# First projections taken by weight piece, no filler matmuls, chunk 1's input turned by DMA, score runs joined, and a new order for a fused attention and ReGLU block

## The chip, the cores and the metric

One core of a Trainium2 chip runs the kernel. The metric is the device time in microseconds (us) of one execution; the kernel before has a median of 191.26 us over three runs (191.16 to 192.79). The engines are PE (matmul), DVE (vector), ACT (scalar activation, which also copies PSUM to SBUF here), POOL (here mostly the issuer of accumulating DMAs) and SP (issuer of the other DMAs). Each engine works through its own instructions strictly in the order of the program and waits on semaphores for the others.

## What is computed

```python
def _A_ref(x, wqkv, wo):                      # S = 2048 tokens, D = 512, 32 heads of 16
    q, k, v = ...                             # x @ wqkv, by heads
    off = jnp.arange(8) * 2                   # each token sees 8 tokens: 0, 2, ... 14 back
    kg, vg = k[..., idx_c, :], v[..., idx_c, :]
    logits = jnp.einsum("bhsd,bhswd->bhsw", q, kg) * scale
    attn = _softmax(where(mask, logits, -1e9))
    o = jnp.einsum("bhsw,bhswd->bhsd", attn, vg)
    return o @ wo
def _B_ref(x, W_gate, W_up, W_down):          # F = 1376
    return (relu(x @ W_gate) * (x @ W_up)) @ W_down
h  = x + _A_ref(_layernorm(x), wqkv, wo)
h2 = h + _B_ref(_layernorm(h), W_gate, W_up, W_down)
```

All tensors are bf16; the sums in PSUM are fp32.

## The kernel before

**Tiling.** The 2048 tokens are four chunks of 512, called 0 to 3. For each chunk the work is: layer norm of x (statistics on DVE, L467 and L470; Ln and Exp for the reciprocal root on ACT, L480 and L484; the normalised row in token order, L515 on DVE for chunk 0 and L512 on ACT for the rest), four tokens-by-features blocks of 128 rows, called x0 to x3 of the chunk; the turn to features-by-tokens, either on PE against an identity (L544) with a copy out of PSUM (L560 on ACT, L558 on DVE for one block), or by a transposing DMA from SP (L533); twelve projection groups of 4 x 512 columns (L585: four for q, four for k with `wqk_sb`, four for v with `wv_sb`), copied out by ACT (L593); the products of q with the eight shifted k on DVE (L636, and L651 in halves for chunk 0; L680 adds two of them beforehand); the scores as column-tiled matmuls against `sel` (L642, L694); Exp (L708); the denominator (L725, L731, L734); the weights scaled by its reciprocal (L752) and spread over the partitions by DMA (L768), four transfers from SP or POOL for each half of the eight offsets; the products with v on DVE (L800, L815), whose sum is begun by an accumulating DMA from POOL (L843) and ended on DVE (L803, L837, L807); the output projection (L881), the residual (L892), the second layer norm (L457, L510, turned by DMA at L533); gate and up (L954, the last 96 features in L921), their product (L982) and down (L1005).

**The start.** The loads of x0 to x3 of chunk 0 and of the q/k weight come in pieces: SP issues x0, x2, x3 and x4, ACT issues x1 and the first three of the four row blocks of the weight (pieces 0 to 2), SP later the fourth. PE runs 77 matmuls on zeros meanwhile (L428), and 8 more behind the turn of x1 (L436, the fillers). The first six of the twelve groups of chunk 0 are issued in parts of 128 or 256 columns and of two weight pieces at a time, so that each part waits only for the columns and the pieces that it reads.

**What sets the order.** A planner (`Plan`) holds every step with its engine, an estimated time and what it needs; the list `RANK` gives each step its place. Loads that the planner does not issue have estimated arrival times in `XT` (x) and `WT` (weights). Its estimates set no waits on the chip: they only choose the order of each engine's instructions and the buffers. Nearly everything that follows, then, is `RANK`.

**Late loads.** `LATE = "ud"` names weights that the planner loads: up and down, behind chunk 0's attention (`lg`, L861). The down loads have one more condition in the plan, chunk 1's spreads (`op.deps += abd`). The gate weights are loaded in the setup (L349).

Of the kernel before, what the change touches and what calls it, by code (L numbers as in the profile page):

```python
# [201 lines left out]
def kernel(  # L202
# [24 lines left out]
    PRE2 = ()  # L227
    PRD = ()
    ODA = (0, 1)
    LATE = "ud"  # L230
    NAB = 0
    SCALE = DH ** -0.5
    EPS = 1e-5
# [72 lines left out]
    def f_load(n, i):  # L306
        if n == "d":
# [3 lines left out]
            if FTAIL and i:  # L311
                nc.sync.dma_start(wd_sb[:FTAIL, NFF, :], B_W_down[NFF * P:F, :])
# [76 lines left out]

    MERGE = (0, 1, 2, 3)  # L390

    BCN = 4

    HG = ([[0, 1, 2, 3]],) * 4
    HSP = ()
# [699 lines left out]
```

## Time and profile before

| | us |
|---|---|
| median of the three runs (lowest, highest) | 191.26 (191.16, 192.79) |
| span of the profiled execution, first to last instruction | 190.2 |
| PE busy | 185.1 (97%) |
| DVE busy | 150.7 (79%) |
| ACT busy | 113.5 (60%) |
| POOL busy | 25.2 (13%) |

The profile is of one execution; its span is 1.06 us under the median of the runs, and the runs do not list the profiled one apart. PE is busy from the first microsecond to 187.3, but "busy" holds the 85 matmuls on zeros, and the end of each matmul is modelled with its latency. DVE is full up to about 125 us and light after that. ACT is nearly full between 16 and 38 us. The granted clock of PE reads 1.00 in every slice of the page but the last.

### The profile page before, as it was taken

The numbers are of one execution on the slowest core, as the hardware profiler recorded it, in microseconds if no ns is written. First come the engines' busy times: TensorE is split into PE (matmuls) and PEld (weight loads), VectorE is DVE, ScalarE is ACT, GpSimd is POOL, SyncE is SP. The second block draws the span as 40 slices with busy tenths as digits, with TensorE's granted clock in tenths as the row PEclk, the third lists the DMA queues.
The fourth block names the chain that finished last, engine by engine and source line by source line (L and its number), as shares of the span: only waits on it lengthen the run. The fifth ranks groups of instructions, "written<-read, shape, count | busy, mean of one in ns | idle before, by whom it ended". The sixth has DMA issues, their size and how long they took to land.

```text
span 190.2 us, 3080 instructions
## 1 busy us (share of the span) xinstructions
PE 185.1 (97%) x1127; PEld 95.4 (50%) x1127; DVE 150.7 (79%) x231; ACT 113.5 (60%) x234; POOL 25.2 (13%) x47
## 2 busy tenths in 40 slices
PE   7799999999999999999999999999999999999993
PEld 7676555554444445544344464444454444455453
DVE  5899999999999999999999998998485712114324
ACT  2579999985467945762483795146466713358500
POOL 4000221400000004230033123027000000000000
PEclk9999999999999999999999999999999999999999
DMA  5999364993198858998438798779922211000503
GB/s 182 281 347 370 90 163 87 191 194 59 21 330 177 233 166 153 194 191 182 83 65 152 142 181 186 180 137 166 221 44 55 55 28 59 28 0 0 165 3 110
DMA packets 27743, 26.98 MB, mean 142 GB/s; under 512 B 14704, under 2 KB 23248, under 8 KB 27728
## 3 DMA queue, kind: packets, MB, share of 16 engines
q1 hardware_dynamic: 23696, 15.34, 29.7%
q0 software_dynamic: 3312, 10.49, 28.6%
q10 hardware_dynamic: 720, 0.95, 1.5%
q8 instruction: 9, 0.15, 0.3%
q14 instruction: 6, 0.05, 0.1%
HBM read 8.42 MB, written 2.10 MB: 55 GB/s over the span
## 4 chain that ended last, share of the span: by engine, by line
PE 82%; ACT 11%; DMA 3%; DVE 1%; issue 1%; SPq 0%
PE bank L954 37%; PE bank L1005 20%; PE bank L585 12%; PE bank L881 7%; ACT row L512 5%; DMA x_sm<-in_A_x_dram 3%; PE bank L921 3%; ACT quad L560 2%; ACT vT L593 2%; PE bank L642 2%; ACT quad L593 1%; PE bank L694 1%; ACT kT L593 1%; ACT ex L708 1%; SPq L323 0%
## 5 line engine op out<-in xcount | busy, mean ns | idle before, releaser
L954 PE MATMUL bank<-quad,wgu_sb 128*128 128x512 bf16 x320 | 72.3, 379 | 0.0
L954 PEld LDWEIGHTS <-wgu_sb 128*128 128x128 bf16 x320 | 30.9, 98 | 37.3 <-issue 1.7
L1005 PE MATMUL bank<-wd_sb,gT 128*128 128x512 bf16 (+3 forms) x198 | 39.7, 355 | 0.0
L958 ACT CAST up_sb<-bank 128x512 bf16<-128x512 f32 x40 | 23.1, 591 | 21.0 <-PE bank L954 14.9
L585 PE MATMUL bank<-quad,wqk_sb 128*128 128x512 bf16 (+2 forms) x176 | 30.4, 321 | 0.5 <-DVE quad L558 0.4
L961 ACT ACTIVATE gr<-bank 128x512 bf16<-128x512 f32 x40 | 23.3, 606 | 9.7 <-PE bank L954 8.2
L1005 PEld LDWEIGHTS <-gT 128*128 128x128 bf16 (+1 forms) x198 | 18.5, 98 | 19.7
L982 DVE TENSOR_TENSOR gT<-gr,up_sb 128x1024 bf16<-128x1024 bf16 x20 | 13.6, 686 | 14.4 <-PE bank L1005 7.0
L636 DVE TENSOR_TENSOR big<-quad,kT 128x4096 bf16<-128x4096 bf16 x11 | 24.8, 2279 | 0.0
L585 PEld LDWEIGHTS <-wqk_sb 128*128 128x128 bf16 x176 | 17.1, 113 | 11.4 <-issue 1.1
L800 DVE TENSOR_TENSOR big<-big,vT 128x4096 bf16<-128x4096 bf16 x9 | 20.4, 2281 | 0.0
L843 POOL DMA_DIRECT2D big<-big x13 | 11.6, 965 | 64.3 <-PE bank L954 32.6
L1013 DVE SCALAR_TENSOR_TENSOR row<-bank,iv,x_sm 128x512 bf16<-128x512 f32 (+2 forms) x10 | 6.3, 643 | 13.4 <-PE bank L1005 13.2
L457 ACT ACTIVATE junk<-x_sm,sm 128x512 bf16<-128x512 bf16 x16 | 11.6, 727 | 8.8 <-DVE x_sm L892 8.8
L585 PE MATMUL bank<-quad,wv_sb 128*128 128x512 bf16 x64 | 16.1, 380 | 0.2 <-ACT quad L560 0.2
L881 PE MATMUL bank<-wo_sb,quad 128*128 128x512 bf16 x64 | 15.0, 379 | 0.0
L892 DVE SCALAR_TENSOR_TENSOR x_sm<-x_sm,bank 128x512 bf16<-128x512 bf16 x16 | 10.8, 678 | 2.4 <-PE bank L881 2.4
L803 DVE TENSOR_TENSOR big<-big 128x1024 bf16<-128x1024 bf16 (+1 forms) x17 | 10.3, 622 | 1.6 <-DMA big<-big 1.4
L467 DVE BATCH_NORM_STATS2 st<-x_sm 128x6 f32<-128x512 bf16 x16 | 10.2, 679 | 1.1 <-DMA x_sm<-in_A_x_dram 1.1
L593 ACT CAST quad<-bank 128x512 bf16<-128x512 f32 x16 | 9.3, 594 | 2.5 <-PE bank L585 2.4
L593 ACT CAST kT<-bank 128x512 bf16<-128x512 f32 x16 | 9.3, 596 | 1.9 <-PE bank L585 1.0
L593 ACT CAST vT<-bank 128x512 bf16<-128x512 f32 x16 | 9.1, 610 | 2.1 <-PE bank L585 2.1
(80 smaller groups left out, 175.6 us busy)
## 6 DMA issues: line engine op xcount, KB each, us to landing
big<-big POOLq DMA_DIRECT2D x13, 512.0 KB, 5.2
big<-ex SPq DMA_DIRECT2D x20, 128.0 KB, 3.1
big<-ex POOLq DMA_DIRECT2D x12, 128.0 KB, 3.8
wgu_sb<-in_B_W_gate_dram SPq DMA_DIRECT2D x1, 1376.0 KB, 9.3
wgu_sb<-in_B_W_up_dram SPq DMA_DIRECT2D x2, 688.0 KB, 5.0
wd_sb<-in_B_W_down_dram SPq DMA_DIRECT2D x2, 640.0 KB, 5.7
x_sm<-in_A_x_dram SPq DMA_DIRECT2D x2, 512.0 KB, 6.2
wqk_sb<-wqk_sb POOLq DMA_DIRECT2D x2, 512.0 KB, 5.8
```

Of the source, the lines that this page charges most:

```text
L457: nc.scalar.activation(out=junk[:, j % 2, :], in_=h.t[:] if h else x_sm[:, tk * BPC + j, :], func=ACT.Square, bias=sm.t[:, j:j + 1], scale ...
L585: nc.tensor.matmul(mm.t[:, lo:hi], lhsT=wv_sb[:, dt, t:D:NT] if c == 2 else wqk_sb[:, dt, c * D + t:(c + 1) * D:NT], rhs=xnT.t[:, dt, lo:h ...
L593: nc.scalar.copy(out=o, in_=mm.t[:])
L636: V.tensor_tensor(out=pb.t[:].rearrange("p (t w) s -> p t w s", t=2), in0=q4, in1=k4, op=ALU.mult)
L800: V.tensor_tensor(out=mt.t[:], in0=ab.t[:], in1=v8, op=ALU.mult)
L843: nc.gpsimd.dma_start(mt.t[:, 0:4, :], mt.t[:, 4:8, :], accum_op=ALU.add)
L881: nc.tensor.matmul(od.t[:], lhsT=OT.t[:, t, j * P:(j + 1) * P], rhs=wo_sb[:, t, :], start=(t == 0), stop=(t == NT - 1 and tk not in RPE))
L954: nc.tensor.matmul(mm.t[:fs, lo:hi], lhsT=wgu_sb[:, dt, g, ft * P: ft * P + fs], rhs=hnT.t[:, dt, lo:hi], start=(dt == 0), stop=(dt == NT ...
L958: nc.scalar.copy(out=ub.t[:fs, i, :], in_=um.t[:fs, :])
L961: nc.scalar.activation(out=gr.t[:fs, i, :], in_=gm.t[:fs, :], func=ACT.Relu)
L982: V.tensor_tensor(out=gt.t[:fs, 0:n, :], in0=gr.t[:fs, 0:n, :], in1=ub.t[:fs, 0:n, :], op=ALU.mult)
L1005: nc.tensor.matmul(od.t[:, c0:c1], lhsT=gts[ft].t[:fs, ft % 2, j * P:(j + 1) * P], rhs=wd_sb[:fs, ft, c0:c1], start=(ft == 0), stop=(ft == ...
```

## The change

Six things, of which the last moves nearly every row.

1. The first six groups of chunk 0 are issued in smaller parts: the first 128 columns with weight piece 0 alone ("a"), then piece 1 ("f"), the next 128 columns with pieces 0 and 1 ("d"), and 256 columns with piece 2 ("g") and piece 3 ("h"). Each part waits in the plan for the piece that it reads (`WP`).
2. The eight fillers are gone (`NFILL`).
3. The copy of the turned x1 goes from DVE to ACT (`TEV = ()`).
4. The normalised rows of chunk 1 are turned by four transposing DMAs on SP instead of 16 PE transposes and two ACT copies (`('x',1,0)` and `('x',1,2)` in `DMAT`).
5. The two score runs of a chunk are issued as one, in chunks 1 to 3 (`MS`).
6. The gate load becomes a planned step (`LATE = "udg"`); the down loads lose their condition (`LDD = 0`); the arrival estimates and `RANK` are new.

```diff
-    LATE = "ud"
+    LATE = "udg"
...
+        elif n == "g":
+            nc.sync.dma_start(wgu_sb[:, :, 0, :], B_W_gate.rearrange("(dt p) f -> p dt f", p=P))
...
-        nc.sync.dma_start(wgu_sb[:, :, 0, :], B_W_gate.rearrange("(dt p) f -> p dt f", p=P))
-
+        if "g" not in LATE:
+            f_load("g", 0)
...
-    NWARM, NFILL = (62, 15), (8, 0, 0)
+    NWARM, NFILL = (62, 15), (0, 0, 0)
...
-    XT = (3.45, 3.65, 4.05, 5.3, 7.15, 8.65, 9.0, 9.4, 13.0, 14.5)
-    WT = (8.35, 8.35, 7.0, 10.85, 15.8, 25.5, 19.2, 29.0)
-    DMAT = (('h',0,0),('h',0,2),('h',2,0),('h',2,2),('h',3,0),('h',3,2),('h',1,0),('h',1,2),('x',3,0),('x',3,2))
+    QD = 6
+    XT = (3.5, 3.7, 4.6, 6.3, 7.3, 8.3, 8.6, 8.95, 13.1, 14.5)
+    WT = (7.95, 7.95, 6.2, 11.2, 15.8, 25.5, 19.2, 29.0)
+    WP = (4.4, 6.2, 7.15, 7.95)
+    DMAT = (('h',0,0),('h',0,2),('h',2,0),('h',2,2),('h',3,0),('h',3,2),('h',1,0),('h',1,2),('x',1,0),('x',1,2),('x',3,0),('x',3,2))
...
+    MS = (1, 2, 3)
+    LDD = 0
...
+    TEV = ()
...
-                tev = not residual and tk == 0 and j0 == 1
+                tev = not residual and tk == 0 and j0 in TEV
...
-                parts = [("a", 0, P, 0, 2, xev[0:1]), ("d", P, 2 * P, 0, 2, xev[1:2])] if n < QA else [("a", 0, 2 * P, 0, 2, xev[0:2])]
-                parts += [("b", 0, 2 * P, 2, NT, [])]
+                if n < QD:
+                    parts = [("a", 0, P, 0, 1, xev[0:1]), ("f", 0, P, 1, 2, []), ("d", P, 2 * P, 0, 2, xev[1:2]), ("g", 0, 2 * P, 2, 3, []), ("h", 0, 2 * P, 3, 4, [])]
...
-                            evs + [wload["ab"][0] if i in "ad" else wl, a, fills[-1]], pr - 5,
+                            evs + wpc[d0:d1] + [a, fills[-1]], pr - 5,
...
+                if tk in MS:
+                    both.append((sc, ex, [a], [prd[0][1]], nu, f_sc))
...
+            elif tk in MS:
+                both.append((sc, ex, [a for a, _, _ in prd], [b for _, b, _ in prd], 4, lambda p=prd: [f() for _, _, f in p]))
...
+            if tk in MS and hf == 0:
+                continue
+            if tk in MS:
+                a = add(("sc1", tk), "PE", sum(x[4] for x in both) * MM + SW, lambda p=both: [x[5]() for x in p],
+                        [d for x in both for d in x[2]], apr, take=[x[0] for x in both], use=[d for x in both for d in x[3]], lat=PEL)
...
-        if tk == 1 and "d" in LATE:
+        if tk == 1 and "d" in LATE and LDD:
             for op in wload["d"]:
                 op.deps += abd
```

How the order moves is read from the two programs themselves. In the rows, `x_sm` is the input, `st` and `mv` the statistics, `rs` the reciprocal root, `row` a normalised block.

**The start on DVE.** Before, the piece with the first normalised rows (`row_104` is x0, `row_105` x1, `row_106` x2, `row_107` x3; `st_116` is the statistic of x3):

```order
L467 BN_STATS st_114<-x_sm 128x6
L470 BN_AGGR mv_117<-st_114 128x2
L515 TENSOR_SCALAR row_104<-x_sm,mv_117,rs_129 128x512
L467 BN_STATS st_115<-x_sm 128x6
L515 TENSOR_SCALAR row_105<-x_sm,mv_117,rs_129 128x512
L470 BN_AGGR mv_117<-st_115 128x2
L467 BN_STATS st_116<-x_sm 128x6
L470 BN_AGGR mv_117<-st_116 128x2
L558 COPY quad_79<-bank_140 128x4x128
L515 TENSOR_SCALAR row_106<-x_sm,mv_117,rs_129 128x512
```

And in the changed program:

```order
L480 BN_STATS st_115<-x_sm 128x6
L483 BN_AGGR mv_117<-st_114 128x2
L483 BN_AGGR mv_117<-st_115 128x2
L528 TENSOR_SCALAR row_104<-x_sm,mv_117,rs_129 128x512
L480 BN_STATS st_116<-x_sm 128x6
L483 BN_AGGR mv_117<-st_116 128x2
L528 TENSOR_SCALAR row_105<-x_sm,mv_117,rs_129 128x512
L528 TENSOR_SCALAR row_106<-x_sm,mv_117,rs_129 128x512
L528 TENSOR_SCALAR row_107<-x_sm,mv_117,rs_129 128x512
```

The row of x1 stood ahead of the statistic of x3 and stands behind it now; the row of x0 stands behind the statistic of x2.

**The start on PE.** In the changed program the end of the turn of x2 and the first projections stand so (`bank` are PSUM banks, `quad_79` is the turned x of chunk 0):

```order
L557 LDWEIGHTS row2_106
L557 MATMUL bank3_141<-identity_61,row2_106 128x128
L598 LDWEIGHTS wqk_sb_72
L598 MATMUL bank4_142<-quad0_79,wqk_sb_72 128x128
L598 LDWEIGHTS wqk_sb_72
L598 MATMUL bank5_143<-quad0_79,wqk_sb_72 128x128
```

Before, fourteen projection matmuls stood ahead of the turn of x2; now the turns of x0, x1 and x2 all stand ahead of the first one.

**Chunk 1's weights on DVE.** Before, the piece from the scaling of the weights (L752; `ex_102` and `ex_100` are the two halves, which the spreads then copy) to the first product with v (L800):

```order
L636 TENSOR_TENSOR big_92<-quad_87,kT 128x4096
L752 TENSOR_TENSOR ex_102<-ex_102,rec_103 128x512
L752 TENSOR_TENSOR ex_100<-ex_100,rec_103 128x512
L636 TENSOR_TENSOR big_89<-quad_87,kT 128x4096
L636 TENSOR_TENSOR big_88<-quad_87,kT 128x4096
L636 TENSOR_TENSOR big_90<-quad_87,kT 128x4096
L680 TENSOR_TENSOR big_92<-big_92,big_88 128x4096
L800 TENSOR_TENSOR wqk_sb<-big_91,vT 128x4096
```

And in the changed program:

```order
L653 TENSOR_TENSOR big_88<-quad_87,kT 128x4096
L783 TENSOR_TENSOR ex_102<-ex_102,rec_103 128x512
L653 TENSOR_TENSOR big_91<-quad_87,kT 128x4096
L783 TENSOR_TENSOR ex_100<-ex_100,rec_103 128x512
L653 TENSOR_TENSOR big_92<-quad_87,kT 128x4096
L697 TENSOR_TENSOR big_88<-big_88,big_91 128x4096
L1013 TENSOR_TENSOR gT_93<-gr_112,up_sb_109 128x1024
L831 TENSOR_TENSOR wqk_sb<-big_89,vT 128x4096
```

Between the second scaling and the first product stood four instructions of 4096 elements; now there stand two, and one of 1024. On SP the down loads follow chunk 1's eight spreads in both programs.

More of the change, by code (lines that the diff above doesn't have):

```diff
@@ L419 @@
         wload[n] = []
+    wpc = [load(t) for t in WP]
     wload["q"][0].take.append(qkb)
@@ L430 @@
     fills = [add(("warm", 0), "PE", 5.6, f_warm, [], -500, take=[wb])]
+    if "g" in LATE:
+        wload["g"].append(add(("ldg", 0), "SP", 0.45, lambda: f_load("g", 0), wload["o"], 0, lat=1.0, dq=(1.0, 3.6)))
     def fill(d, k):
@@ L510, in f_xn @@
                     V.tensor_scalar(out=xn.t[:], in0=x, scalar1=float(D), scalar2=sm.t[:, j:j + 1], op0=ALU.mult, op1=ALU.subtract)
-                elif on_act:
+                elif on_act and (ln, tk, j) not in XND:
                     nc.scalar.activation(out=xn.t[:], in_=x, func=ACT.Identity,
@@ L621 @@
         kp = {t: kdone.get((tk - 1, t)) for t in range(NT)}
+        both = []
         for hf in range(2):
@@ L696, in f_sc @@
                                              stop=(u == nu - 1), tile_position=(0, g * HB))
[L698 removed]
+                if tk in MS:
+                    both.append((sc, ex, [a], [prd[0][1]], nu, f_sc))
+                else:
+                    scd = [add(("sc%d" % hf, tk), "PE", nu * MM + SW, f_sc, [a], apr, take=[sc], use=[prd[0][1]], lat=PEL)]
+            elif tk in MS:
+                both.append((sc, ex, [a for a, _, _ in prd], [b for _, b, _ in prd], 4, lambda p=prd: [f() for _, _, f in p]))
             elif tk in MERGE:
@@ L705, with f_ex, f_mk @@
                                    take=[sc], use=[pb], lat=PEL))
-            def f_ex(sc=sc, ex=ex):
-                nc.scalar.activation(out=ex.t[:], in_=sc.t[:], func=ACT.Exp, scale=SCALE)
-            def f_mk(hf=hf, ex=ex):
-                V.tensor_tensor(out=ex.t[:, 0:PADL], in0=ex.t[:, 0:PADL], in1=mask[:, hf, :],
-                                op=ALU.mult)
-            a = add(("ex%d" % hf, tk), "ACT", A5, f_ex, scd, apr, take=[ex], use=[sc], lat=AL)
-            if tk == 0:
-                a = add(("mk%d" % hf, tk), "DVE", DSM, f_mk, [a], apr, use=[ex], lat=DL)
-            exs.append(ex)
-            exd.append(a)
+            if tk in MS and hf == 0:
[3 more added lines that the diff above has]
+                        [d for x in both for d in x[2]], apr, take=[x[0] for x in both], use=[d for x in both for d in x[3]], lat=PEL)
+                scs = [(h, x[0], x[1], [a]) for h, x in enumerate(both)]
+            else:
+                scs = [(hf, sc, ex, scd)]
+            for h, sc, ex, scd in scs:
+                def f_ex(sc=sc, ex=ex):
+                    nc.scalar.activation(out=ex.t[:], in_=sc.t[:], func=ACT.Exp, scale=SCALE)
+                def f_mk(h=h, ex=ex):
+                    V.tensor_tensor(out=ex.t[:, 0:PADL], in0=ex.t[:, 0:PADL], in1=mask[:, h, :],
+                                    op=ALU.mult)
+                a = add(("ex%d" % h, tk), "ACT", A5, f_ex, scd, apr, take=[ex], use=[sc], lat=AL)
+                if tk == 0:
+                    a = add(("mk%d" % h, tk), "DVE", DSM, f_mk, [a], apr, use=[ex], lat=DL)
+                exs.append(ex)
+                exd.append(a)
         dn, rc = Buf(at_s), Buf(rc_s)
```

13 lines of the change are left out of this document (8 added, 5 removed), and 76 rows, old and new, of the table RANK.

## The prediction

> **What bounds the kernel now.** I read the page, then the chain of waits, then windows and the timeline.
>
> ```profile
> span 190.2 us, 3080 instructions
> PE 185.1 (97%) x1127; PEld 95.4 (50%) x1127; DVE 150.7 (79%) x231; ACT 113.5 (60%) x234; POOL 25.2 (13%) x47
> ...
> 16.00:38.00 22.00, 21.84 (x148) 11.61 (x146) 21.97 (x35) 21.67 (x39) 5.51 (x8) 1.00 0.66 163
> 38.00:60.00 22.00, 22.00 (x126) 10.54 (x125) 21.96 (x35) 14.03 (x28) 0.39 (x1) 1.00 0.66 153
> 60.00:125.00 65.00, 64.99 (x349) 30.29 (x348) 63.75 (x78) 38.13 (x83) 13.01 (x18) 1.00 0.76 162
> 125.00:187.30 62.30, 62.29 (x330) 30.53 (x327) 29.56 (x48) 30.59 (x66) 4.39 (x5) 1.00 0.34 75
> ```
>
> The window rows give, behind a stretch and its length, the busy time of PE, its weight loads, DVE, ACT and POOL, then the granted clock. From 16 us to 187.3 PE has no hole worth naming, so PE sets the end. But DVE is as full up to 125 us, and its results come to PE just in time:
>
> ```profile
> 47.53 0.76 DVE L807 TENSOR_TENSOR quad<-big,rec 128x512 bf16<-128x512 bf16 x2
> 48.29 3.62 PE L881 MATMUL bank<-wo_sb,quad 128*128 128x512 bf16 x16
> ...
> 84.65 0.42 DVE L837 TENSOR_TENSOR quad<-big 128x512 bf16<-128x512 bf16 x1
> 85.47 2.75 PE L881 MATMUL bank<-wo_sb,quad 128*128 128x512 bf16 x12
> ```
>
> DVE's last input for chunk 0's output projection is done at 48.29 and PE starts on it at 48.29; in chunk 1 it is 85.07 and 85.47. Time taken off PE is kept only if DVE is no later than before. The sum goes against the span of 190.2; the median of the runs lies 1.06 above it, and I add that 1.06 to what I get.
>
> **The start: the first projection comes later, +0.6.** Timeline rows (start, length, engine, line), then two pieces of the chain:
>
> ```profile
> 0.99 4.81 PE L428 MATMUL bank<-warm 128*64 128x64 bf16 x77 [0.99 <-DVE warm L327]
> 5.77 0.40 PE L544 MATMUL bank<-identity,row 128*128 128x128 bf16 x4
> 6.23 0.40 DVE L515 TENSOR_SCALAR row<-x_sm,mv,rs 128x512 bf16<-128x512 bf16 x1
> 6.92 0.61 PE L436 MATMUL bank<-warm 128*128 128x128 bf16 x8
> 7.33 0.69 DVE L467 BATCH_NORM_STATS2 st<-x_sm 128x6 f32<-128x512 bf16 x1 [0.61 <-DMA x_sm<-in_A_x_dram]
> 7.37 0.83 PE L585 MATMUL bank<-quad,wqk_sb 128*128 128x128 bf16 x12
> 8.06 0.18 DVE L470 BATCH_NORM_AGGREGATE mv<-st 128x2 f32<-128x6 f32 x1
> 8.46 0.79 DVE L515 TENSOR_SCALAR row<-x_sm,mv,rs 128x512 bf16<-128x512 bf16 x2
> 8.60 0.27 PE L585 MATMUL bank<-quad,wqk_sb 128*128 128x128 bf16 x2 [0.40 <-DVE quad L558]
> ...
> 10.48 5.54 PE bank L585 x54
> ...
> 19.96 0.61 PE L544 MATMUL bank<-identity,row 128*128 128x128 bf16 x8
> 20.41 1.03 PE L585 MATMUL bank<-quad,wv_sb 128*128 128x512 bf16 x4
> ```
>
> The row of x1 was made at 6.23, before DVE waited for x3, which lands at 7.30; its statistic starts at 7.33. In the new order of DVE that row stands behind the statistic of x3, and on PE the turns of x0, x1 and x2 stand ahead of the first projection. So: x3's statistic and aggregation end at 8.24, the rows of x1 and x2 take 0.40 each (0.79 for two), 9.0, and the turn of x2 four matmuls. Eight turns last 0.45 us (19.96 to 20.41), 0.056 each, so 9.2 for the first projection, against 7.37 before. The smaller parts let "a" start when piece 0 of the weight is there, but the turn of x2 now stands in front, so this gives nothing here. Before, 14 matmuls of 128 columns were done by 8.87, 14 x 0.056 = 0.78 us of work, which now lies behind 9.2. Part of that lead was lost again before, as PE is dense only from 10.48. So between 0.4 and 0.8 is lost: I take 0.6.
>
> **The clock: +1.4.** The fillers and the early projections kept PE at work between 5.8 us and 9.2; now that stretch of 3.4 us holds three turns, 12 matmuls or 0.67 us. So I compare stretches of about that length:
>
> ```profile
> 5.23:8.64 3.41, 2.50 (x39) 2.08 (x37) 2.77 (x9) 1.90 (x8) 0.00 (x0) 1.00 0.96 322
> 186.14:189.50 3.36, 1.15 (x16) 0.93 (x14) 1.22 (x4) 0.00 (x0) 0.00 (x0) 1.00 0.51 156
> 189.50:190.20 0.70, 0.00 (x0) 0.00 (x0) 0.00 (x0) 0.00 (x0) 0.00 (x0) 0.53 0.00 0
> ...
> L428 PE MATMUL bank<-warm 128*128 128x128 bf16 x15 | 1.4, 264 | 0.0
> L436 PE MATMUL bank<-warm 128*128 128x128 bf16 x8 | 0.6, 219 | 0.0
> ```
>
> With PE busy 2.50 of 3.41 us (73%) the clock stays at 1.00. At the end, 1.15 busy in 3.36 (34%) are followed by 0.53 on the mean, so by half the clock from about 189.54. In the changed kernel 5.23 to 8.64 holds the end of the warm matmuls (to 5.80, 0.57) and one turn (0.40, as the row at 5.77 counts one): 0.97 of 3.41, 28%, which lies on the side that falls. Coming back takes dense work: the last 15 warm matmuls still have a mean of 264 ns where the fillers have 219, so the clock rose only some 4 us after the first matmul at 0.99. The cost is half of the time that PE works at half clock: none if it holds, 2.1 if it takes 4.2 us again. I take as long as the quiet stretch, 3.4 us from 8.64, of which PE has work from 9.2 on: 2.8 us, 1.4 lost. DVE's first products wait for these projections and move with them, so nothing behind absorbs it.
>
> [...]
>
> **Off PE: turns and score runs, -1.2.** Sixteen turns of chunk 1 go, 16 x 0.056 = 0.9. For the score runs the chain has:
>
> ```profile
> 67.90 0.98 PE bank L642 x16
> 68.88 0.43 PE bank L694 x8
> ...
> 94.28 0.55 PE bank L694 x8
> ```
>
> Eight score matmuls cost 0.55 alone and 0.43 behind another run. In chunk 2 the two runs stand together already; chunks 1 and 3 win 0.12 each by these rows, 0.2 if entering the run costs the like. I take 0.3 for both, so -1.2 in all, bounds -1.1 and -1.3. ACT has two copies fewer in 16 to 38 us; PE is full there too, so I count nothing beyond the turns (bound: 1 us of gain).
>
> **DVE and the queues: +0.2.** Rows on the spreads, the turns and the gate weights:
>
> ```profile
> 20.30 4.84 SPq L768 DMA_DIRECT2D big<-ex  x4
> 57.48 5.11 SPq L768 DMA_DIRECT2D big<-ex  x8
> 59.10 8.80 PE L954 MATMUL bank<-quad,wgu_sb 128*128 128x512 bf16 x40
> 81.70 4.18 SPq L768 DMA_DIRECT2D big<-ex  x4
> 85.98 1.26 SPq L940 DMA_TRANSPOSE gT<-row  x1
> ...
> big<-ex SPq DMA_DIRECT2D x20, 128.0 KB, 3.1
> wgu_sb<-in_B_W_gate_dram SPq DMA_DIRECT2D x1, 1376.0 KB, 9.3
> quad<-row SPq DMA_TRANSPOSE x20, 2.5
> ...
> L636 DVE TENSOR_TENSOR big<-quad,kT 128x4096 bf16<-128x4096 bf16 x11 | 24.8, 2279 | 0.0
> L982 DVE TENSOR_TENSOR gT<-gr,up_sb 128x1024 bf16<-128x1024 bf16 x20 | 13.6, 686 | 14.4 <-PE bank L1005 7.0 <-ACT up_sb L958 4.0 <-ACT gr L961 3.4
> ```
>
> In chunk 1 two large instructions and a small one now stand between the second scaling of the weights and the first product: 2 x 2.28 + 0.69 = 5.2 us; before there were four large ones, 9.1. The second half's four transfers need three issues of 0.64 (5.11 for eight) and 3.1 to land, 5.0. In chunk 2 three large ones remain, 6.8; SP first turns a last row (1.26), then issues at 1.05 each (4.18 for four): 1.26 + 3.15 + 3.1 = 7.5, so 0.7 late. If DVE is later, PE's next output projection is, with what little stands ahead of it. Bounds 0 and 2.0 (0.7 in each of chunks 1 to 3, taken as lost in full); I take 0.2, since PE comes later by the start as well.
>
> Chunk 1's four transposing DMAs go ahead of chunk 0's spreads on SP; SP gets the weights at 20.30 before, and PE turned chunk 1's rows at 19.96, so the rows are there by then and the last turned block lands by 19.96 + 2.5 = 22.5. PE's full row from 16 to 38 us hides it if other projections stand ahead; if not, up to 2.5 us show. The gate load goes from the setup to behind four spreads and four more turns, by the rows 20.30 + 4.84 + 4 x 1.26 = 30.2, and lands 9.3 later at 39.5, 19 us ahead of its first use at 59.10; the down loads keep their place on SP; the copy of x1 falls into ACT's wait (0.58 if not). All at nothing.
>
> **Sum.** 190.2 + 0.6 + 1.4 - 1.2 + 0.2 = 191.2 of span, 192.26 with the 1.06: **192.2 us**, 0.5% above the median and within the 1% that a measurement of this kernel can tell from no change.
>
> **Rivals.**
>
> *The clock holds.* [...] Against: 28% against 34%. It gives 190.2 + 0.6 - 1.2 + 0.2 = 189.8, so **190.8 us**.
>
> *The spreads come late, and slower it is.* One mechanism: DVE stands before the first product with v in chunks 1 to 3, its full queue behind it, and PE behind that. For it: 5.2 against 5.0, 6.8 against 7.5 us, and PE with no reserve at 48.29 and 85.47. Against: PE has one projection group more ahead of chunk 0's output projection than before, and by my sum it is there 2 us later itself. It decides as soon as the transfers land over 1 us behind the scaling plus the two products. With the upper bound of 2.0 for 0.2 and the clock as in my sum: **194.1 us**.
>
> *The parts do what they say.* If x3 lands 1 us earlier (the planner's table has 6.3, the trace 7.30), the first projection is at 8.2, the quiet stretch is 2.4 us, the clock holds and the start costs 0.6 - 1.0 = -0.4: 190.2 - 0.4 - 1.2 + 0.2 = 188.8, **189.8 us**; with the gain on ACT up to 1 us more. Against: no load ahead of x3 changes on its queue.
>
> **Chances.** My sum 0.43 (own range 191.3 to 193.3), the clock holds 0.25, late spreads 0.20, the parts work 0.12. Faster by over 1%, under 189.35: half of the last and a quarter of the second, 0.12. Slower by over 1%, over 193.17: nine tenths of the third and a fifth of the first, 0.26. Within: 0.62. The range from 189.4 to 194.4 leaves out the best cases of the last rival and the worst of the third, 2 in 10.
>
> **What would show it.** Right: the first projection at about 9.2, behind x3's statistic; a clock of 0.5 in a stretch between 8 and 13 us; no turns of chunk 1 on PE; 32 or 24 score matmuls in one piece; DVE's wait before L831 under 1 us in each chunk. Wrong: a first projection near 7.4, a clock of 1.00 throughout, or PE with holes of over 1 us behind 40 us, which would put DVE in charge.

## The result and the profile after

| | median (lowest to highest), us | ratio to before, 95% interval |
|---|---|---|
| before, beside the change | 191.41 (191.16 to 192.79) | |
| the change | 210.21 (207.42 to 212.61) | 1.092 (1.084 to 1.101) |

The change is 18.8 us slower by the medians, 9.2% or 17.7 us by the ratio. The forecast was 192.2, with a range from 189.4 to 194.4: the time is 16 us above the upper end. The runs of the change also lie further apart: 5.2 us where those of before lie within 1.6. The medians here and below hold every run and the ratios leave out those over 1.5% above the fastest of their kernel, so where the two differ the text goes by the ratios, and e3 and e10, with one run left each, have none.

The page of the changed kernel, then the first three of the windows that the prediction shows of before:

```profile
span 208.2 us, 3019 instructions
PE 187.8 (90%) x1084; PEld 95.6 (46%) x1103; DVE 150.1 (72%) x230; ACT 112.1 (54%) x233; POOL 25.2 (12%) x47
```

```profile
16.00:38.00 22.00, 21.59 (x131) 10.91 (x133) 19.97 (x34) 18.98 (x37) 5.88 (x8) 1.00 0.71 145
38.00:60.00 22.00, 17.65 (x104) 8.51 (x105) 19.03 (x28) 10.38 (x21) 0.00 (x0) 1.00 0.63 161
60.00:125.00 65.00, 59.13 (x300) 26.89 (x305) 56.88 (x61) 37.18 (x79) 10.82 (x14) 0.95 0.70 146
```

DVE's work is what it was (150.1 us against 150.7), but it now stands still for 2 us before 38, 3 more before 60 and 8 before 125 where it stood still for 1.3 in all. PE has holes of 4.4 and 5.9 us in the last two windows, where it had none. The lists of waits name them (engine, what waits for what, us in total, times, longest; the rows that bear on the holes):

```profile
DVE big L834 <- DMA big<-big: 7.3, 4, 4.0
DVE big L831 <- DMA wqk_sb<-ex: 3.8, 1, 3.8
DVE big L831 <- PE bank L711: 2.4, 1, 2.4
```

```profile
PE bank L985 <- issue: 5.3, 1, 5.3
PE bank L912 <- DVE quad L838: 3.2, 1, 3.2
PE bank L952 <- DMA quad<-row: 3.0, 1, 3.0
```

**First place, 31 to 53 us.** POOL's accumulating DMAs for chunk 0 before, then the timeline of the change:

```profile
32.18 0.92 POOL L843 DMA_DIRECT2D big<-big  x1 [6.88 <-PE bank L585]
33.30 0.88 POOL L843 DMA_DIRECT2D big<-big  x1 [0.20 <-issue]
36.66 1.73 POOL L843 DMA_DIRECT2D big<-big  x2 [2.49 <-DVE row L740]
```

```profile
30.89 0.92 POOL L874 DMA_DIRECT2D big<-big  x1 [5.74 <-PE bank L598]
31.09 0.58 SPq L314 DMA_DIRECT2D wgu_sb<-in_B_W_gate_dram  x1
32.87 0.88 POOL L874 DMA_DIRECT2D big<-big  x1 [1.06 <-DVE big L846]
35.38 1.74 POOL L874 DMA_DIRECT2D big<-big  x2 [1.63 <-DVE big L846]
39.99 0.69 DVE L834 TENSOR_TENSOR big<-big 128x1024 bf16<-128x1024 bf16 x1 [4.02 <-DMA big<-big]
52.66 2.76 PE L912 MATMUL bank<-wo_sb,quad 128*128 128x512 bf16 x12 [3.18 <-DVE quad L838]
```

The issues of DMAs between 10 and 60 us (count, size, median time to landing), of before and then of the change:

```profile
big<-big POOLq DMA_DIRECT2D x4, 512.0 KB, 5.9
```

```profile
big<-big POOLq DMA_DIRECT2D x4, 512.0 KB, 10.8
wgu_sb<-in_B_W_gate_dram SPq DMA_DIRECT2D x1, 1376.0 KB, 13.6
```

The gate load now starts 0.2 us behind the first of chunk 0's four accumulating DMAs. These take nearly twice as long, DVE waits 4.0 us for the first, and the output projection of chunk 0 starts at 52.66 instead of 48.29.

**Second place, 92 to 107 us.** Before, chunk 2's weights were scaled at 80 us, and the first product with v came at 98.25:

```profile
79.73 0.40 DVE L752 TENSOR_TENSOR ex<-ex,rec 128x512 bf16<-128x512 bf16 x1
81.27 0.41 DVE L752 TENSOR_TENSOR ex<-ex,rec 128x512 bf16<-128x512 bf16 x1
98.25 2.29 DVE L800 TENSOR_TENSOR big<-big,vT 128x4096 bf16<-128x4096 bf16 x1
```

In the change:

```profile
92.19 6.53 SPq L546 DMA_TRANSPOSE quad<-row  x4
95.75 0.75 DVE L783 TENSOR_TENSOR ex<-ex,rec 128x512 bf16<-128x512 bf16 x2
96.81 2.23 POOL L799 DMA_DIRECT2D wqk_sb<-ex  x4 [14.42 <-DVE ex L783]
99.32 4.37 SPq L799 DMA_DIRECT2D wqk_sb<-ex  x4
103.77 6.40 PE L985 MATMUL bank<-quad,wgu_sb 128*128 128x512 bf16 x16 [5.33 <-issue]
106.89 4.49 DVE L831 TENSOR_TENSOR big<-wqk_sb,vT 128x4096 bf16<-128x4096 bf16 x2 [3.78 <-DMA wqk_sb<-ex]
```

The transposing DMAs of chunk 1's second norm, from issue to landing (least, median, most), before and then in the change:

```profile
DMA to landing us min/median/max: 2.4/2.4/2.5
```

```profile
DMA to landing us min/median/max: 3.4/4.0/6.3
```

Chunk 2's weights are now scaled at 95.75. POOL issues its four spreads from 96.81 on, and SP the fourth turn at 97.39; the turn lands at 103.7, and PE, which the list shows behind "issue", stands still for 5.3 us until then. SP's spreads are behind the turns, and DVE waits 3.8 us for them. Behind the hole the granted clock is half:

```profile
98.45:103.77 5.32, 0.00 (x0) 0.03 (x1) 4.66 (x3) 3.88 (x10) 1.50 (x3) 0.89 0.98 166
103.77:109.60 5.83, 5.83 (x15) 2.10 (x16) 2.71 (x2) 0.00 (x0) 0.00 (x0) 0.51 0.47 134
```

At 141 us the same happens with chunk 2's fourth turn (3.0 us), beside an accumulating DMA. Output projections start at 52.7, 88.4, 129.9 and 163.0 (before: 48.3, 85.5, 117.7, 142.5).

### The profile page after: what moved, and what is told of

Read it like the earlier page. It is cut to its first block, busy times and chain, and to the rows that moved or that the text cites. A ratio compares the mean times of both kernels' runs of the same rounds, so it can differ in the third digit from the quotient of the medians.

```text
span 208.2 us, 3019 instructions
## 1 busy us (share of the span) xinstructions
PE 187.8 (90%) x1084; PEld 95.6 (46%) x1103; DVE 150.1 (72%) x230; ACT 112.1 (54%) x233; POOL 25.2 (12%) x47
## 4 chain that ended last, share of the span: by engine, by line
PE 42%; DVE 28%; DMA 18%; issue 7%; SPq 2%; ACT 1%; POOL 0%; DVEq 0%; ACTq 0%; POOLq 0%
PE bank L985 27%; PE bank L1036 9%; DMA big<-big 6%; DMA big<-ex 5%; DVE big L653 4%; DMA quad<-row 4%; DVE big L668 4%; DVE x_sm L923 3%; DVE big L846 3%; DMA x_sm<-in_A_x_dram 2%; DVE big L831 2%; DVE wqk_sb L831 2%; DVE gT L1013 2%; PE bank L598 2%; DVE big L834 2%
## 5 line engine op out<-in xcount | busy, mean ns | idle before, releaser
L985 PE MATMUL bank<-quad,wgu_sb 128*128 128x512 bf16 x312 | 75.2, 394 | 5.9 <-issue 5.3
L985 PEld LDWEIGHTS <-wgu_sb 128*128 128x128 bf16 x320 | 32.0, 101 | 45.5 <-issue 12.2
L1036 PE MATMUL bank<-wd_sb,gT 128*128 128x512 bf16 (+4 forms) x193 | 39.8, 355 | 1.1 <-DMA gT<-row 0.9
L598 PE MATMUL bank<-quad,wqk_sb 128*128 128x512 bf16 (+2 forms) x172 | 29.9, 320 | 0.4 <-DMA quad<-row 0.2
L653 DVE TENSOR_TENSOR big<-quad,kT 128x4096 bf16<-128x4096 bf16 x12 | 27.3, 2280 | 0.0
L834 DVE TENSOR_TENSOR big<-big 128x1024 bf16<-128x1024 bf16 (+2 forms) x19 | 12.5, 660 | 7.4 <-DMA big<-big 7.3
L831 DVE TENSOR_TENSOR big<-wqk_sb,vT 128x4096 bf16<-128x4096 bf16 x4 | 9.1, 2288 | 6.2 <-DMA wqk_sb<-ex 3.8
L831 DVE TENSOR_TENSOR big<-big,vT 128x4096 bf16<-128x4096 bf16 x6 | 13.5, 2284 | 0.0
L1042 ACT ACTIVATE up_sb<-bank,iv 128x512 bf16<-128x512 f32 x8 | 5.4, 688 | 13.5 <-PE bank L1036 13.5
L912 PEld LDWEIGHTS <-quad 128*128 128x128 bf16 x64 | 6.1, 98 | 10.9 <-DVE quad L838 3.4
## 6 DMA issues: line engine op xcount, KB each, us to landing
wgu_sb<-in_B_W_gate_dram SPq DMA_DIRECT2D x1, 1376.0 KB, 13.6
```

Source lines behind the costliest of these rows:

```text
L598: nc.tensor.matmul(mm.t[:, lo:hi], lhsT=wv_sb[:, dt, t:D:NT] if c == 2 else wqk_sb[:, dt, c * D + t:(c + 1) * D:NT], rhs=xnT.t[:, dt, lo:h ...
L653: V.tensor_tensor(out=pb.t[:].rearrange("p (t w) s -> p t w s", t=2), in0=q4, in1=k4, op=ALU.mult)
L831: V.tensor_tensor(out=mt.t[:], in0=ab.t[:], in1=v8, op=ALU.mult)
L834: V.tensor_tensor(out=mt.t[:, 0:n, :], in0=mt.t[:, 0:n, :], in1=mt.t[:, n:2 * n, :], op=ALU.add)
L912: nc.tensor.matmul(od.t[:], lhsT=OT.t[:, t, j * P:(j + 1) * P], rhs=wo_sb[:, t, :], start=(t == 0), stop=(t == NT - 1 and tk not in RPE))
L985: nc.tensor.matmul(mm.t[:fs, lo:hi], lhsT=wgu_sb[:, dt, g, ft * P: ft * P + fs], rhs=hnT.t[:, dt, lo:hi], start=(dt == 0), stop=(dt == NT ...
```

## The experiments

Two groups: parts of the change undone in the changed kernel, and parts done alone in the kernel before. `move(steps, behind)` puts steps behind another one in the order in which the program issues them. Prices are against the kernel before timed beside them (medians 191.8 to 192.1). Line numbers shift by one or more between the kernels with edits; the tile names tell the step.

### The gate load: e1, e2, e3

e1, in the changed kernel:
```diff
-        if "g" not in LATE:
-            f_load("g", 0)
+        f_load("g", 0)
...
-... lambda: f_load("g", 0), wload["o"], ...
+... lambda: None, wload["o"], ...
```


> The changed kernel with the gate load issued in the setup, as before the change; everything else is the changed kernel. Theory A, collision: the 1376 KB gate load at 31.09 us runs beside chunk 0's four accumulating DMAs, which take 10.8 us in the median where they took 5.9 before; DVE waits 4.0 us for the first, the output projection of chunk 0 starts at 52.7 where it started at 48.3, and the rest of the 18 us follows from that. Then this kernel falls to 189 to 195 us, with accumulating DMAs near 6 us. Theory B, order: the new order has too little between the steps of DVE and PE, and the load only adds to it. Then this kernel stays above 203 us, with PE holes at about 100 and 140 us as in the changed kernel.

Measured: 203.44 us (201.12 to 210.01), ratio 1.049 (1.046 to 1.053). Of the 9.2% by which the change is slower 4.3% come back, 8.2 us, and 4.9% stay, 9.4 us (6.8 and 11.5 by the medians). Neither theory alone: the load is nearly half of the loss, and the order holds the rest.

e2, in the kernel before:
```diff
-        nc.sync.dma_start(wgu_sb[:, :, 0, :], B_W_gate...)      # setup
...
         for op in todo:
             ...
+            if op is tds[3]:                                    # fourth turn of chunk 3's x
+                nc.sync.dma_start(wgu_sb[:, :, 0, :], B_W_gate...)
```


> The kernel before with one edit: the gate load leaves the setup and is issued on SP behind the four turns of chunk 3's input, at about 32 us, where the changed kernel has it. Theory A: the accumulating DMAs of chunk 0 go from 5.9 to about 10 us, the output projection of chunk 0 comes 2 to 5 us later, and the time is 195 to 207 us. Theory B: the old order has a product of chunk 1 between chunk 0's last product and the first sum, which covers 2.3 us of the delay, so the time stays within 191 to 194 us.

Measured: 196.26 us, ratio 1.022 (1.018 to 1.026): 4.2 us for this step alone. Chunk 0's output projection starts at 52.2, 3.9 later, and DVE's wait for accumulating DMAs (the row below; 1.4 us before) is where theory A puts it:

```profile
DVE big L802 <- DMA big<-big: 5.5, 4, 3.0
```

e3 has two of the four row blocks in the setup:
```diff
+        nc.sync.dma_start(wgu_sb[:, 0:2, 0, :], ...[:, 0:2, :])          # setup
...
-            nc.sync.dma_start(wgu_sb[:, :, 0, :], ...)
+            nc.sync.dma_start(wgu_sb[:, 2:4, 0, :], ...[:, 2:4, :])
```


> The changed kernel with two of the four row blocks of the gate weights (688 KB) loaded in the setup and the other two where the changed kernel has them. Theory A: half the bytes collide, so the accumulating DMAs lie between 6 and 10.8 us and the time between that of the gate load in the setup and 210, about 197 to 203. Theory B: no change against the changed kernel, 206 to 211.

Measured: 207.06 us (201.19 to 209.96). The median lies between, but the runs lie too far apart for a verdict.

### The second and third place: e5, e6, e9, e10, e7

e5, with the gate load in the setup:
```diff
+    move(ex1, ops("ex0", 2)[0])
+    move(es, ops("tree3", 1)[1])
+    move(den, ops("dn2", 0)[0])
+    move(dr, ops("ge5", 0)[0])
+    move(ops("am1", 2) + ops("am0", 2) + ops("bd1P", 2), ops("tree1", 1)[1])
```


> The changed kernel with the gate load in the setup, and with chunk 2's denominator, scaling and the four spreads on POOL moved ahead of chunk 1's residual, some 7 us earlier; SP's four spreads stay behind the turns. Theory C, turns caught: with the gate in the setup PE still idles 5.3 to 6.0 us at about 98 us, because the fourth turn of chunk 1's second norm is issued while POOL's spreads start, and lands 6.3 us after its issue where turns landed in 2.4 to 2.5 before the change; PE has nothing else in its queue, and its clock is then at 0.50 for 6 us, 3 us more. With POOL's spreads out of the way the turns land in 2.5 to 3.5, the hole is under 2 us, the clock stays at 1.00 there, and the time falls from 201 to 194 to 197. Rival D, DVE late: the hole comes from the rows, which DVE delivers 1.1 us later behind the output projection than before, and from too little work on PE; then the hole stays at 4 us or more and the time at 199 to 204.

Measured: 201.33 us, ratio 1.042 (1.032 to 1.052). PE's 5 us hole is gone: two waits of 1.3 (for a PSUM bank that my move took) and 0.8 are left. But the ratio is only 0.7% under that of e1, and the intervals overlap: no gain of its own is shown. DVE still waited 2.9 us for SP's half of the spreads, and e8 below agrees that most of the hole was room that PE had anyway.

e6 adds one move:
```diff
+    move(ops("ta2", 3), ops("oa1", 1)[0])
```


> As the kernel before, and the first accumulating DMA of chunk 3 on POOL goes behind the first one of the output (138.0 to about 142.5 us), out of the way of chunk 2's fourth turn, which landed 5.0 us after its issue where the three ahead of it landed in 2.4. Theory C: the second hole (3.0 us at 141 us, with a clock of about 0.8 behind it) shrinks to under 1 us and 3 to 5 us more come off: 190 to 194 us. Rival D: no change against the kernel before this one, within 1 us.

Measured: 199.55 us, ratio 1.031 (1.021 to 1.041). The wait of 3 us at 141 us (L952 in the change) is gone (0.5 us of it in e9, which keeps this move), and 1.8 us come off in the median; the intervals of e5 and e6 overlap. Both moves together, against e1, are clear: 1.049 to 1.031, 3.6 us.

e9 gives SP's half of chunk 2's spreads to POOL:
```diff
-    BCD = {... (2,0):"SSSS", ...}
+    BCD = {... (2,0):"PPPP", ...}
...
-    move(ops("am1", 2) + ops("am0", 2) + ops("bd1P", 2), ...)
+    move(ops("am1", 2) + ops("am0", 2) + ops("bd1P", 2) + ops("bd0P", 2), ...)
```


> As the kernel with the early scaling and the late accumulating DMA, and chunk 2's other four spreads go from SP, where they stood behind the turns, to POOL, right behind its first four. Theory C': what DVE waits for decides up to about 145 us; it still waits 3.3 us before chunk 2's first product with v, for SP's spreads, which land at 103.3. Without that wait 2 to 4 us come off: 194 to 197 us in the median, and no wait of DVE for spreads in chunk 2. Rival D: PE has little more to do there whatever DVE does, the wait moves to another of DVE's inputs, and the time stays within 1 us of 199.6.

Measured: 200.03 us, ratio 1.037 (1.030 to 1.044). DVE's wait for spreads is gone, and no time: rival D. The waits that are left in it:

```profile
DVE big L833 <- DMA big<-big: 6.1, 3, 4.1
DVE big L830 <- PE bank L710: 2.4, 1, 2.4
```

The second is the joined score run of chunk 3: DVE's next product needs a buffer that this run reads, and PE comes to it only behind 15 groups of gate and up.

e10 moves a store on SP behind the turns:
```diff
+    move(late, ops("htd", 2)[3])        # late: the store of chunk 0's second half
```


> As the kernel before it, and on SP the store of chunk 0's second half goes behind the four turns of chunk 2's second norm; it waited there for an accumulating DMA, and the first turn was issued 3 us after its row was made. If the turns set chunk 2's gate and up, another 1 to 3 us come off, and the first turn follows its row within 1.5 us; if DVE's products set it, nothing, within 1 us.

Measured: 199.93 us (196.37 to 200.68), no ratio. No difference that can be told.

e7 has the moves of e5 and e6, and the gate load where the change has it (the two edits above on the changed kernel).

> The changed kernel, gate load where the change has it (31 us), with both moves of the kernel before. Theory A and C together: each is paid by itself, so this is 4 to 9 us above that one, 195 to 202 us. Rival: the gate load alone would give the whole loss back through the later holes, then 206 us or more.

Measured: 204.25 us, ratio 1.067 (1.059 to 1.074). This is 3.6% or 7.0 us above e6 (4.7 by the medians), within the 4 to 9 us that were expected, though above the 195 to 202 us; the rival falls. In the changed order the gate load costs 7 to 8 us by the ratios (e7, e1; 5 to 7 by the medians), in the old order 4.2 (e2).

### The clock behind the hole: e8

```diff
+    def busy(f=hole.fn, b=hole.take[0]):
+        for _ in range(20):
+            nc.tensor.matmul(b.t[:], lhsT=warm[:], rhs=wv_sb[:, 0, :], start=True, stop=True)
+        f()
```
(in the kernel of e1, ahead of chunk 1's first gate and up)

> The changed kernel with the gate load in the setup and 20 matmuls of 512 columns without use (4.3 us) on PE in front of the first gate and up projection of chunk 1, where PE idles 5.3 to 6.0 us. They take no time that PE would use. If half the clock behind the hole costs time, the clock stays at 1.00 between 102 and 110 us and the time falls by about 3 us, from 201 to 197 to 199; if the wait alone counts, the time stays at 201 to 202.

Measured: 202.00 us (201.34 to 205.89), ratio 1.053 (1.046 to 1.061), as e1. The clock stays at 1.00 and the hole is filled, but the time that PE gains it loses in the next window, where it waits again:

```profile
100.00:120.00 20.00, 20.00 (x115) 9.51 (x114) 16.46 (x15) 12.64 (x25) 4.25 (x5) 1.00 0.74 149
120.00:140.00 20.00, 15.81 (x83) 7.60 (x82) 17.28 (x26) 3.75 (x8) 4.89 (x7) 1.00 0.84 162
```

So half the clock there cost nothing that could be measured: up to about 145 us PE waits for what DVE and the DMAs deliver, sooner or later. This is one hole, and the start (e12) is another case.

### The start: e4, e12, e13, e16

e4, in the kernel before:
```diff
-            for _ in range(k):
+            for _ in range(0):
```


> The kernel before without its eight filler matmuls (0.45 us of PE work behind the turn of x1). My forecast had the clock fall to half at about 8.6 us without them and the early projections, for 1.4 us; here the fourteen early projections remain, so the stretch from 5.23 to 8.64 has about 1.9 of 3.41 us busy. Theory of the forecast: clock 1.00 or a fall, 191 to 193 us. Rival: PE's clock does not care, and the fillers only delay the first projection by a few tenths: 190.5 to 191.5.

Measured: 191.17 us (190.84 to 191.61) against 192.11, ratio 0.995 (0.993 to 0.997). The rival is right: the fillers cost 0.9 us. This kernel is faster than both, by half a percent against before.

e12, on e4:
```diff
+    move(ops("xst3", 0) + ops("xag3", 0), ...)      # ahead of x1's row on DVE
```


> The kernel before without fillers and with x1's normalised row on DVE behind the statistic of x3, as the change has it. My forecast put the first projection 1.8 us later for this, 0.6 us of the time, and a fall of the clock for 1.4 more. By the forecast: against the kernel without fillers alone (191.2 us) the time grows to 191.8 if the clock holds and to about 193 if it falls, and the runs spread more than 1 us, since the start then follows the landing of x3, which was between 6.6 and 8.3 us in the profiles so far. Rival: PE catches up, since ACT's copies set the pace behind 10 us, and the time stays at 190.9 to 191.5.

Measured: 192.75 us (191.58 to 194.77, twelve runs), ratio 1.004 (1.001 to 1.007): 1.6 above e4, the runs 3.2 us apart where those of e4 lie within 0.8. In the trace of the change the granted clock changes in steps of 3.41 us: it is at half for two of them (102.62 to 109.45 us) and for one (143.58 to 147.00), with ten at full between. Its record starts with a rise, at 7.05 us in the profiled execution of the change (four turns take 0.63 us ahead of it, eight 0.72 behind it) and at 5.12 in that of e12. Stretches of 3.41 us from there on, of the change and then of e12:

```profile
7.05:10.46 3.41, 2.44 (x38) 2.35 (x39) 3.38 (x9) 2.29 (x6) 0.00 (x0) 1.00 0.88 285
10.46:13.87 3.41, 3.36 (x36) 2.79 (x35) 3.09 (x9) 3.17 (x8) 0.00 (x0) 1.00 1.08 383
```

```profile
5.12:8.53 3.41, 1.07 (x19) 0.90 (x17) 2.28 (x7) 1.22 (x4) 0.00 (x0) 1.00 0.99 345
8.53:11.95 3.42, 3.42 (x33) 3.26 (x31) 3.14 (x8) 1.70 (x6) 0.00 (x0) 0.50 0.89 290
```

In e12 PE is busy for 1.07 of 3.41 us (31%), and the next stretch has 0.50. In the profiled execution of the change it is busy for 2.44 (72%), and the next has 1.00. The first projection comes at 8.58 in the change and at 8.56 in e12, so x3's landing is not what differs. The rise does: in the change the matmuls on zeros and the first turn ran on until 6.65 us, so that PE's pause before the next turn is 1.4 us long, not 2.3 as in e12, and the rise at 7.05 lies inside it. The runs of e12 show what the half clock costs: six have a granted clock of 1.00 over the whole run and a median of 191.95 us; five have 0.991, which by that mean is about 3.5 us at half (2 x 0.009 x 192), and a median of 193.88, 1.9 more. The six are 0.1% above before and so 1.1 us above e4, which is the price of the late row alone.

e13, on e10, and e16, on the change itself:
```diff
+    move(ops("xxn1", 0) + ops("xxn2", 0), ops("xre2", 0)[0])
+    move(ops("xst3", 0), ops("xxn2", 0)[0])
```


> As the kernel with the store behind the turns (gate load in the setup, chunk 2's scaling early, all its spreads on POOL, one accumulating DMA late), and on DVE the rows of x1 and x2 go ahead of the statistic of x3, as the kernel before has the row of x1. Theory E, start: in the profiles of this family x3 landed between 6.6 and 8.3 us and the first projection at 8.3 to 10.4, with the clock at half in a stretch behind it; the runs of one kernel spread 4 us and more. With the rows ahead the first projection comes at 7.3 to 8.0 whatever x3 does, the clock stays at 1.00, the runs lie within 1.5 us, and the median falls from 199.9 to 195 to 197.5. Rival: the spread comes from somewhere else, and both stay.

> The changed kernel with only the rows of x1 and x2 ahead of the statistic of x3. Theory E: the spread of the runs (207.4 to 212.6) shrinks to 2 us, and the median falls by 1.5 to 4 us, to 206 to 208.7, since DVE and PE have no reserve against a late start. Rival: the gate load and the spreads make a wait later that takes the start's gain up: 209 to 211.

Measured: e13 197.04 us (196.48 to 198.60), ratio 1.028 (1.023 to 1.033). All four runs have a granted clock of 1.00, where those of e10 have 0.974 to 0.991, and they lie 2.1 us apart instead of 4.3. The median is 2.9 below that of e10, but the fastest run of e10 (196.37) is as fast as those of e13; against e9, the last kernel with a ratio, 0.9% come off, and the intervals overlap. e16 209.31 us (207.96 to 210.17), ratio 1.090 (1.085 to 1.095): the runs come together (2.2 us instead of 5.2, four runs each), and the time is where the rival had it: 0.9 off the median, 0.2% by the ratios, no difference that can be told. So theory E is borne out for the spread; that the start costs the change anything in the median is not shown.

### The fourth part alone, and sums: e11, e14, e17, e20, e18

e11, in the kernel before:
```diff
+    move(ops("am0", 2) + ops("am1", 2) + ..., ops("hxn", 1)[3])   # ...: chunk 2's spreads on POOL
+    move(ops("bd0S", 2), ops("htd", 1)[3])
```


> The kernel before with one edit: chunk 2's scaling of the weights goes from 80 us to behind chunk 1's last normalised row (about 92 us), and SP's four spreads of it behind the turns, as the change has them. Theory C': DVE then waits 3 to 6 us for the spreads before chunk 2's first product with v (98.25 us before), the fourth turn may land late, and the time is 194 to 199 us. Rival D: the old order has enough between, 191 to 193 us.

Measured: 195.31 us, ratio 1.018 (1.015 to 1.021): 3.5 us. Waits of DVE and of PE that the kernel before does not have:

```profile
DVE big L800 <- DMA big<-ex: 2.3, 1, 2.3
PE bank L954 <- DMA quad<-row: 2.0, 2, 1.2
```

e14, on e4:
```diff
+                    if (ln, tk) == ("x", 1):
+                        nc.sync.dma_start_transpose(out=dst.t[:, :, j * P:(j + 1) * P], in_=xn.t[:])
```
(behind each normalised row of chunk 1; the 16 turns and two copies are left out)

> The kernel before without fillers, and chunk 1's rows turned by four transposing DMAs on SP instead of 16 turns on PE and two copies on ACT, the change's fourth part alone. By the forecast PE loses 0.9 us of work, and SP is free there: 190.2 to 190.6 us against 191.2. Rival: the turned rows land later than PE and ACT made them (2.5 to 4 us behind each row), the four transfers collide with the late loads of x and of the gate weights, and the gain is lost: 191.2 to 193.

Measured: 198.07 us (196.77 to 198.72), ratio 1.031 (1.026 to 1.035). Not a gain of 0.9 but a loss of 6.9 against e4. Rows of its timeline:

```profile
16.62 2.93 ACT L512 ACTIVATE row<-x_sm,nb,rs 128x512 bf16<-128x512 bf16 x4
17.46 5.41 SPq L523 DMA_TRANSPOSE quad<-row  x4
22.96 2.85 SPq L776 DMA_DIRECT2D big<-ex  x4
25.39 1.03 PE L593 MATMUL bank<-quad,wv_sb 128*128 128x512 bf16 x4 [3.22 <-DMA quad<-row]
```

ACT makes the rows at 16.6 to 19.6, the last turn lands by 25.4, PE waits 3.2 us, and chunk 0's spreads, which SP issues from 19.56 on in e4, stand behind the turns until 22.96. Behind PE's wait the granted clock is at half for about 3.4 us, by its mean of 0.83 between 20 and 30 us, so the 6.9 hold what that costs.

e17 is e4 with the edits of e2, e11 and e12; e18 has that of e14 as well; e20 is e4 with those of e14 and e2.

> The kernel before without fillers and with three edits at once: gate load at about 32 us, chunk 2's scaling and spreads behind chunk 1's rows, x1's row behind x3's statistic. If the three only add: 191.2 + 4.2 + 3.4 + 1.6 = 200.4, 199 to 202 us. If each delay uses up the reserve that hides the next, more: 203 to 208. If the later delays are taken up by the waits that the gate load makes anyway: 196 to 198.

> The kernel before without fillers, with chunk 1's rows turned by DMA and the gate load behind chunk 3's turns (about 32 us). If the turn's 6.9 us come from the gate load that runs beside the turns at 17 to 25 us, the turned rows now land in 2.4 to 3 us, PE waits under 1 us for them, and the time is 195 to 198, close to that of the late gate load alone (195.4 without fillers). If they come from the rows, which ACT makes at 16.6 to 19.5 us in this order, and from the spreads behind the turns on SP, PE still waits 2 us or more and the time is 199 to 203.

> The kernel before without fillers and with four edits: gate load at about 32 us, chunk 2's scaling and spreads late, x1's row behind x3's statistic, and chunk 1's rows turned by DMA. If the four add, 191.2 + 4.2 + 3.4 + 1.6 + 6.9 = 207.3, 205 to 210 us, near the changed kernel's 210. If the turn by DMA costs less once the gate load is out of its way, 202 to 205. If the delays hide each other, under 202.

| | measured | above before | sum of its parts |
|---|---|---|---|
| e2 gate load late | 196.26 | 4.2 | |
| e11 chunk 2's scaling late | 195.31 | 3.5 | |
| e12 x1's row late, no fillers | 192.75 | 1.0 | |
| e14 turn by DMA, no fillers | 198.07 | 6.3 | |
| e17 = e2 + e11 + e12 | 200.96 | 9.2 | 8.6 |
| e20 = e2 + e14 | 202.18 | 10.3 | 10.4 |
| e18 = all four | 208.33 | 16.4 | 15.9 (the fillers' 0.9 taken once) |
| the change | 210.21 | 18.8 | |

By the ratios the column "above before" reads 4.3, 3.5, 0.7, 5.9, 9.4 (sum 8.4), 10.2 (10.1), 17.2 (15.3) and 17.7. So the four add within 0.6 us by the medians and within 2 by the ratios, which is as far as the interval of e18 (1.079 to 1.100) can tell. The 6.9 us of the turn come from the rows and the queue and not from the gate load beside it: in e20, where that load is out of the way, PE waits the same 3.2 us, and the time is the plain sum.

The kernel before with these four edits is within 2 us of the changed one, but that is in part luck, since the two don't lose their time in the same places. Windows of e18, then one of the change (its window from 16 to 38 us is above):

```profile
16.00:38.00 22.00, 18.44 (x106) 8.55 (x105) 18.33 (x32) 16.36 (x31) 4.18 (x6) 0.92 0.54 122
125.00:145.00 20.00, 20.00 (x105) 9.75 (x103) 18.22 (x32) 10.89 (x26) 5.66 (x10) 1.00 0.78 166
```

```profile
125.00:145.00 20.00, 16.01 (x80) 7.79 (x79) 19.00 (x30) 4.96 (x10) 4.89 (x7) 0.96 0.82 166
```

Between 16 and 38 us PE stands still for 3.6 us in e18, where it waits for the turned rows, and for 0.4 in the change. Between 125 and 145 us it is the other way round: nothing in e18, 4.0 in the change. So the price of e14 is not paid at its place in the change, while the gate load costs more there (e1, e7) than e2 says.

## Why the prediction was wrong

**What bounds the kernel.** It said that time taken off PE is kept only if DVE is no later, with 48.29 and 85.47 as places without reserve. That was right, and it then priced DVE at 0.2.

**DVE and the queues, +0.2 (bounds 0 and 2.0): the step that failed.** Of the gate load it asked only whether it lands before its first use. It does (44.7 against 64.03). It did not ask what the 1376 KB run beside, though POOL's accumulating DMAs stood at 32 to 37 us before, in the same window: put at nothing, this costs 4.2 us in the old order (e2) and, by the ratios, 7 to 8 in the changed one (e1, e7). The row of the load in the setup gave 9.3 us to landing; it took 13.6. In chunk 2 the sum had 6.8 us of DVE against 7.5 for the spreads, 0.7 late. The change took 10.4 from the second scaling (96.5) to the product (106.89): SP issued behind the last turn at 99.32, and a landing of 3.1 us, the median of SP's 20 spreads before, became 5.2 to 6.2, where chunk 2's own had taken 4.3 to 5.3 before. That the fourth turn of the second norm would take 6.3 us instead of 2.5 had no term. The step alone costs 3.5 in the old order (e11). The prediction's own sign of this, PE holes of over 1 us behind 40 us, is what the profile shows.

**Off PE, -1.2.** The 16 turns and the separate runs are gone from PE, as said, and the cover held in the profiled execution of the change: the rows come at 13 to 18 us, PE waits 0.2 for the turned blocks, and DVE's products with v of chunk 0 end at 35.97 (36.13 before). In the old order, with the rows at 16.6 to 19.6, the same swap costs 6.9 against e4; the prediction had up to 2.5 if nothing stood ahead, and no price on the spreads' delay behind the turns. The cover is not safe in the changed order either: in e13, with the gate load back in the setup, PE waits 2.7 for turned rows of x. The joined runs: 0.3 forecast, not run alone.

**The start, +0.6, and the clock, +1.4.** On the kernel before the moved row costs 1.1 where the clock holds and 1.9 more where it falls, as in half of e12's runs. So both terms were near in size there, and that the late row can bring the clock down was right. In the change it was a matter of luck: in its profiled execution the first projection came at 8.58, not 9.2, and the clock held at 1.00, with its rise at 7.05 and not at 5.23 as before, and PE busy for 2.44 of the 3.41 us behind it. That the fillers keep the clock was wrong for the kernel before: without them it holds (0.998 to 1.00 in the ten runs of e4) and gains 0.9. The 28% of the forecast lies below the 31% behind which e12's clock read 0.50. The forecast took 3.4 us at half for a fall; behind PE's hole in the change it lasted 6.83, 102.62 to 109.45.

**The rivals.** Late spreads, with DVE ahead of PE, was the nearest, at 0.20 and 194.1 us. Its price took three small gaps and left out what the late DMAs would meet: each other. The upper end of the range rested on it.

**Open.** From the changed side, e13 is still 5.3 us above before; its profile has PE waits of 2.7 (turned rows of x), 2.2 (the fourth turn) and 1.3 us (the bank of my move), about that sum. The joined score runs and the finer first parts were not tried alone; e9's wait of 2.4 us is the only sign of what the joined runs cost. PE's hole at 141 us in the change has only e6, whose own gain lies within its interval. Why the gate load costs more in the changed order than in the old one stays open too.

## What to carry to other kernels

When a transfer is moved, asking whether it lands before its use is half the question: list what is in flight at its new place, and price those transfers' consumers. In a kernel where two engines are full, a step that is hidden in one order is not hidden in another, so a part's price holds for the order in which it was measured: here 6.9 us, done alone, was not paid at its place in the change, and 4.2, done alone, was 7 to 8 there. Do a part alone and also undo it in the whole. Where PE's hole followed from late DMAs and a late DVE, keeping PE's clock up bought nothing here (e8).

## What the runs showed of the hardware

- A transposing DMA of a 128x512 block landed in 2.4 to 2.5 us in chunk 1's second norm before. In the change the same four took 3.4 to 6.3, the longest the one that was issued among POOL's spreads; in chunk 2 three took 2.4 and the fourth, beside an accumulating DMA, 5.0. Other transfers beside it are not the whole story: the first two at 92 us took 4.4 and 3.6, and the program issued no other transfer between 89 and 96 us.
- Four accumulating DMAs of 512 KB took 5.9 us in the median before, and 10.8 beside the load of 1376 KB in the change.
- The landing of x3, which the same instruction issues at 1.7 us, came at 7.30 us in the profiled execution of before and at 6.7 in that of the change; in that of e14 DVE waits for it until 7.42. An order in which the first projection waits for it had runs 3.2 us apart (e12), the same with a row ahead 0.8 (e4).
- The granted clock of PE in stretches of 3.41 us, counted from the rise in each trace. At full clock, stretches in which PE was busy for 0.00 us (the change, 99.21 to 102.62), 0.47 (the change, 140.17 to 143.58) and 1.07 (e12, 5.12 to 8.53) were followed by one at 0.50, and one with 1.15 (before, 186.14 to 189.50) by 0.53 in the 0.70 us that were left; behind 1.46 (the change, 48.01 to 51.42), 2.44 (the change, 7.05 to 10.46) and 2.50 (before, 5.23 to 8.64) the clock stayed at 1.00. At half clock, 2.27 us busy (the change, 102.62 to 106.04) were followed by another stretch at 0.50, 3.41 (106.04 to 109.45) and 3.32 (143.58 to 147.00) by one at 1.00.
